# A fused attention and two-layer expert kernel: the seven-product blocks in another order, and the layer's inputs loaded during the last expert

## The chip, the cores and the metric

The kernel runs on one core of a Trainium2 chip. The metric is the device time of one execution in microseconds (us). The core has a matrix engine (TensorE, PE in the profile), VectorE (DVE), ScalarE (ACT), GpSimd (POOL) and a queue engine that issues transfers (SP). Each engine runs its instructions strictly in the order in which the program hands them to it, and engines wait for each other by semaphores.

## The reference

Three steps on 1536 tokens of 512 numbers. Local attention gives `x`. A mixture of eight experts follows: every token goes to the expert with the highest gate value, through `relu(x @ w1[e]) @ w2[e]`, and is scaled. Last comes a gated layer without a nonlinearity, and it is this one that the change is about:

```python
def _moe2_ref(x, w_a, w_b, w_out) -> np.ndarray:
    a = x @ w_a            # 1536 x 512 times 512 x 1536
    b = x @ w_b
    return (a * b @ w_out).astype(np.float32)
```

Everything is float32.

## The kernel before, in words

**Precision.** Each float32 matrix is split into a high and a low part (`h`, `l`), and a product is three matmuls: high times high, high times low, low times high. A split is a cast on ScalarE (the high part) and a subtraction on VectorE or GpSimd (the low part).

**Experts.** `for k, n in enumerate(CAPS)` goes through eight experts, k=7 the last. An expert has eight `up` and four `down` products; between them `tick(i)` issues side work for the step i = 0 to 15: loads and splits of later weights (`wstep`, `eload`, `esplit`), and by the table `CV` the first loads and conversions of the last layer's weights. The tokens are sorted by expert, and each expert's results are written transposed to a DRAM scratch `y_dram`. The weights' tiles rotate through pools: of twelve consecutive weight jobs four use pool A and eight pool B.

**The last layer.** Its 1536 tokens are three chunks c = 0, 1, 2 of 512, its 1536 hidden units twelve blocks f of 128. For f = 0 and 1 every chunk is multiplied directly: `first()` does chunk 0 (48 matmuls into the four banks `N0`) as soon as the experts are through, then `plain(c, f, ...)` does chunks 2 and 1. For f = 2 to 11 `seven(f)` computes chunks 0 and 1 together: as two-by-two blocks (a and b against two halves of the inner dimension, times two chunks) with seven products instead of eight, six matmuls each. The seven are, by their operands: `A11`, `S2`, `S1`, `A12`, `S3`, `A22` and `S4`; S1 to S4 are sums of the inputs, T1 to T4 (from `tsum` on VectorE, split by `tsplit` on ScalarE and GpSimd) sums of the weights. Partial sums meet in the banks `pa`, `pb`, `pc` and in the tiles `p1`, `u2`, `u3`. `ab2(0)` and `ab2(1)` are chunk 2's direct products, twelve matmuls each. `gate(c, f, ...)` splits a*b into `gh` (ScalarE) and `gl` (VectorE, when the function that it returns is called).

**Output.** Two neighbouring blocks f are a pair p. `both(p)` puts the pair's twelve output tiles (three chunks of four tiles of 128 tokens) on a list; `fill(n)` takes n tiles off it, each of six matmuls against the output weights in a bank of tag `o` (three of them), then an addition into the accumulator on VectorE (for the first pair a copy, on VectorE or ScalarE by turns).

**Weights.** `JOBS` lists half blocks of weights: for each f two of them, and from f = 2 to 10 one of the output weights (`WO`). A job is loaded by `cload` into one of three stage tiles (SP's queue), unpacked from float64 by `conv1` (two ScalarE operations), `conv2` (three VectorE operations and a GpSimd addition, which frees the stage tile) and split by `conv3` (ScalarE's cast, GpSimd's subtraction). Block f converts the jobs of f+1, `jobs` and `wo`, and loads and unpacks those of f+2, `nxt`.

**The branch.** `with tc.If(rare[0] == 1)` stands between the experts and the last layer: if an expert has more tokens than its capacity, the rest is computed there and the layer's inputs are loaded and prepared again. With these inputs it is not taken, but all five engines go through it, and instructions behind it wait for semaphores that stand in for the branch's own work.

**Order.** The whole program is under `tc.manual_schedule()`: on each engine the order is that of the Python statements. Before the change `xload()` (L1018) loads all three chunks, six transfers of 512 KB, between the last expert and the branch, into `acc`, a tile of a pool that takes the memory of the closed weight pools.

Of the kernel before, what the change touches and what calls it, by code (L numbers as in the profile page):

```python
# [46 lines left out]
def moe_block_kernel(ctx, tc, qd, kd, vd, kt, vn, nv, wg, wg2, we, wm, out):  # L47
# [41 lines left out]
    wA = ctx.enter_context(tc.tile_pool(name="wA", bufs=4))  # L89
    sts = ExitStack()  # L90
# [579 lines left out]
    pools["B"] = wbs.enter_context(tc.tile_pool(name="wB", bufs=8, side="left", reuse_waits="tile"))  # L670
# [64 lines left out]
    def down(W, d, Hm, n, col, pool, bg=None, d0=0, w=CMAX, q=nc.scalar, tag=("h", 6)):  # L735
        Ws = [[x[:, :].rearrange("p (f n) -> p f n", f=2)[:, f % 2, d * P:(d + 1) * P] for x in W(4 + f // 2)] for f in range(8)]
        pp = product(Ws, Hm, n, "ps_y", 255, bg, tag)
        yt = pool.tile([P, w], F32, tag="yt", bufs=4, name="yt")[:, 0:n]
        A.copy(yt, pp[-1])
        if len(pp) == 2:  # L740
            V.tensor_tensor(yt, pp[0], yt, ALU.add)  # L741
        return lambda: q.dma_start(y_dram[d0 + d, :, ds(col, n)], yt)

# [184 lines left out]
    for k, n in enumerate(CAPS):  # L928
# [8 lines left out]
        def tick(i):  # L937
# [28 lines left out]
            for f_, x in CV.get((k, i), ()):  # L966
                f_(x)

# [40 lines left out]
    acc = m1.tile([P, NT, DM], F32, name="acc")  # L1009
    XF = {(c, g): acc[:, 4 * c + 2 * g:4 * c + 2 * g + 2] for c in range(3) for g in range(2)}  # L1010

# [3 lines left out]
    Y2, S4, A22, S1, S2, S3 = (pair(m1, n_, k) for n_, k in (("Y2", 4), ("S4", 2), ("A22", 2), ("S1", 2), ("S2", 2), ("S3", 2)))  # L1015
    A11, A12 = ([y[:, a:a + 2] for y in yT] for a in (0, 2))

    def xload():  # L1018
        for c in (2, 1, 0):
            for g in range(2):  # L1020
                nc.sync.dma_start(XF[c, g], y_dram[2 * g:2 * g + 2, :, c * 512:(c + 1) * 512].rearrange("d p n -> p d n"))

# [7 lines left out]
    xload()  # L1030
    for h, l in (Y2, S4, A22):
        A.copy(h[:, 0, 0:2], ident[:, 0:2])
        V.tensor_copy(l[:, 0, 0:2], ident[:, 0:2])


    with tc.If(rare[0] == 1):
        with ExitStack() as ls:
# [76 lines left out]
            xload()  # L1114
            for g in range(2):
                ysp(XF[0, g], [y[:, 2 * g:2 * g + 2] for y in yT], V)
            first()
# [62 lines left out]
    def out_tile(p, c, t_):  # L1180
# [25 lines left out]
    def seven(f):  # L1206
# [3 lines left out]
        p1, u2, u3 = tmp("p1"), tmp("u2"), tmp("u3")  # L1210
# [5 lines left out]

        def conv_a():
            if jobs:
                conv2(*jobs, *wo)
                for _ in nxt:  # L1220
                    cload(nc.sync)

        def conv_b():
            for j in jobs + wo:
                conv3(j)
            if jobs:
                tsplit(f + 1)

        def ab2(s_):
            pt = bank("ab", 2)  # L1230
            mul(pt, wab(f, s_), Y2, True)
            if s_ == 0:
                A.copy(a, pt)
            else:
                V.tensor_tensor(pt, a, pt, ALU.mult)
                return gate(2, f, pt)

        def p4():
            mul(pb, T4, A22, False, True, True)
            V.tensor_tensor(p1, pb, p1, ALU.add)  # L1240
            V.tensor_tensor(pb, p1, u3, ALU.mult)
            return gate(1, f, pb)

        def p3():
            mul(pc, wab(f, 1, 2, 4), S4, False, True, True)
            V.tensor_tensor(u2, pc, u2, ALU.add)
            V.tensor_tensor(pa, u2, pa, ALU.mult)
            return gate(0, f, pa)
# [3 lines left out]
        conv_a()  # L1252
# [3 lines left out]
        mul(pa, wab(f, 0, 2, 4), A12, False, True, True)  # L1256
        if f % 2:
            ab2(0)
        else:
            fill(2)  # L1260
            if jobs:
                tsum(f + 1)
            fill(2)
            conv_b()
        mul(pb, T3, S3, False, True, True)
        V.tensor_tensor(u3, pb, p1, ALU.add)
        V.tensor_tensor(u3, u3, pc, ALU.add)
        if f % 2:
            if jobs:
                tsum(f + 1)  # L1270
            conv_b()
            low2 = ab2(1)
            low1 = p4()
            low2()
            low0 = p3()
            low1()
            low0()
            for j in nxt:
                conv1(j)
            both(f // 2)  # L1280
            fill(6 if f < 11 else 12)
        else:
            fill(2)
            for j in nxt:
                conv1(j)
            low1 = p4()
            low0 = p3()
            low1()
            low0()
            ab2(0)  # L1290
            ab2(1)()
# [3 lines left out]

    def ssum(o, a, b, op):
        V.tensor_tensor(o, a, b, op)


    def c12(*js):  # L1300
        for j in js:
            conv1(j)
        conv2(*js)
        for _ in js:
            cload(nc.sync)

    c12((12, 0), (12, 1))
    for g in range(2):
        ysp(XF[2, g], [y[:, 2 * g:2 * g + 2] for y in Y2], V)
    evict(0, 0, (N0[0, 0], N0[0, 1]), (), [(conv3, (12, 0)), (ysp, XF[1, 0], S4, V)])  # L1310
    evict(0, 1, (N0[1, 0], N0[1, 1]), (), [(conv3, (12, 1)), (ysp, XF[1, 1], A22, V)])
# [3 lines left out]
    plain(2, 0, ("o", "pc"), [(ssum, XF[1, 1], XF[1, 0], XF[1, 1], ALU.add)],  # L1315
          [(conv1, (2, 0)), (conv1, (2, 1)), (ssum, XF[1, 0], XF[0, 0], XF[1, 0], ALU.subtract)])
    plain(2, 1, ("pa", "pb"), [(conv2, (2, 0), (2, 1)), (cload, nc.sync), (cload, nc.sync)],
          [(ssum, XF[0, 0], XF[1, 1], XF[0, 0], ALU.subtract)])
    plain(1, 0, pab, [(ysp, XF[0, 0], S2, V), (tsum, 2)], [(conv3, (2, 0)), (ssum, XF[0, 1], XF[0, 1], XF[0, 0], ALU.subtract)])
    plain(1, 1, ("o", "pc"), [(conv3, (2, 1)), (tsplit, 2)], [(ysp, XF[1, 1], S1, V)])  # L1320
    both(0)
    ysp(XF[0, 1], S4, V)
    fill(2)
    ysp(XF[1, 0], S3, V)
    fill(4)
    c12((13, 0))
    conv3((13, 0))
    for j in ((3, 0), (3, 1), (13, 1)):
        conv1(j)
    for f in range(2, 12):  # L1330
        seven(f)
# [45 lines left out]
```

## Time and profile before

| | |
|---|---|
| three runs | 623.5, 624.6 and 625.32 us; median 624.6 |
| the profiled execution | 625.51 us, its span 623.8 us, mean granted TensorE clock 0.962 |
| TensorE matmul, busy | 574.1 us, 92% of the span |
| VectorE / ScalarE / GpSimd, busy | 442.2 / 307.7 / 255.2 us |
| DMA | 87.24 MB, mean 140 GB/s |

Times of a row are us from the span's start. A duration is that of one instruction or, with xN, of N merged ones from the first's start to the last's end; instructions on one engine overlap a little at their ends. A bracket `[2.10 <-DVE ...]` is the engine's idle time ahead of the row and what ended it. Matmul ends are modelled. In the rows by stage, the number behind the stage is its length, then busy time and count for each engine, and PEclk is the granted TensorE clock as a share of 2.4 GHz, a mean over the stage.

### The profile page before, as it was taken

How to read it: one execution, taken by the hardware profiler on the slowest of the kernel's cores; microseconds unless marked ns; L12 is line 12 of the kernel's file. 1: busy time of each engine (PE TensorE's matmuls, PEld its weight loads, DVE VectorE, ACT ScalarE, POOL GpSimd, SP SyncE). 2: the span in 40 equal slices, each digit the busy share in tenths (PEclk: the TensorE clock that was granted, in tenths of full speed). 3: DMA queues.
4: the chain of work that ended last, by engine and by line, in shares of the span. 5: the costliest groups of instructions: out<-in, count | busy, mean ns of one | idle time of the engine just before them, and what ended most of it. 6: DMA issues, size and time to landing. Idle time of an engine off the chain costs nothing.

```text
span 623.8 us, 9972 instructions
## 1 busy us (share of the span) xinstructions
PE 574.1 (92%) x3395; PEld 485.8 (78%) x3395; DVE 442.2 (71%) x987; ACT 307.7 (49%) x684; POOL 255.2 (41%) x227
## 2 busy tenths in 40 slices
PE   6998995799999999899979769899999989989995
PEld 4876774799999989889858558678778868868884
DVE  6888886696645868678358567777778678587463
ACT  5786881466566766686245345334234244242110
POOL 3000641543535636454413343743625517346115
PEclk9999997599999999999989779999989989999998
DMA  8476575467657796773831030221303203110004
GB/s 282 148 216 240 170 216 163 145 206 249 222 180 261 226 327 213 238 250 122 285 112 69 0 134 1 101 65 37 102 1 102 100 2 101 35 66 1 0 30 174
DMA packets 38656, 87.24 MB, mean 140 GB/s; under 512 B 5920, under 2 KB 16416, under 8 KB 38592
## 3 DMA queue, kind: packets, MB, share of 16 engines
q1 hardware_dynamic: 31680, 73.55, 36.3%
q0 software_dynamic: 2160, 6.91, 3.1%
q10 hardware_dynamic: 4752, 6.00, 2.9%
q8 instruction: 31, 0.51, 0.4%
q14 instruction: 33, 0.27, 0.1%
HBM read 73.25 MB, written 13.20 MB: 139 GB/s over the span
## 4 chain that ended last, share of the span: by engine, by line
PE 38%; DVE 6%; issue 3%; ACT 1%; POOL 1%; DMA 1%; POOLq 0%; ACTq 0%
PE ps_o L1187 5%; PE ps_o L1185 5%; PE ps_o L1186 5%; PE ps_ab L990 3%; PE ps_ab L989 3%; PE ps_ab L991 3%; PE ps_pb L990 2%; PE ps_pb L989 2%; PE ps_pb L991 2%; PE ps_pa L989 2%; PE ps_pa L991 2%; PE ps_pa L990 2%; PE ps_pc L989 1%; PE ps_pc L991 1%; PE ps_pc L990 1%
## 5 line engine op out<-in xcount | busy, mean ns | idle before, releaser
L886 POOL TENSOR_TENSOR tx<-tx,st 128x512 int32<-128x512 int32 x36 | 57.9, 1633 | 121.6 <-issue 93.1
L110 POOL TENSOR_TENSOR wl<-st,wh 128x512 fp32r<-128x512 f32 x54 | 69.2, 1302 | 91.8 <-ACT wh L105 85.5
L105 ACT CAST wh<-st 128x1024 fp32r<-128x1024 f32 x64 | 67.4, 1054 | 32.5 <-DMA st<-we 31.8
L110 DVE TENSOR_TENSOR wl<-st,wh 128x1024 fp32r<-128x1024 f32 x37 | 53.2, 1439 | 26.7 <-ACT wh L105 26.6
L719 PE MATMUL ps_h<-x,wl 128*128 128x256 f32 (+5 forms) x256 | 69.7, 272 | 0.0
L719 PE MATMUL ps_y<-h,wl 128*128 128x256 f32 (+5 forms) x256 | 68.6, 268 | 0.0
L1187 PE MATMUL ps_o<-wh,gl 128*128 128x512 f32 x144 | 59.7, 415 | 5.2 <-DVE gl L1151 5.2
L1185 PE MATMUL ps_o<-wh,gh 128*128 128x512 f32 x144 | 60.3, 418 | 4.6 <-ACT acc L1190 2.0
L898 POOL TENSOR_TENSOR wl<-tx,wh 128x512 fp32r<-128x512 f32 x36 | 49.5, 1405 | 27.8 <-ACT wh L897 27.8
L1186 PE MATMUL ps_o<-wl,gh 128*128 128x512 f32 x144 | 59.3, 412 | 0.0
L1192 DVE TENSOR_TENSOR acc<-ps_o,acc 128x512 f32<-128x512 f32 x60 | 39.9, 686 | 26.7 <-PE ps_o L1187 26.7
L515 ACT ACTIVATE pe<-pe,mx 128x256 f32<-128x256 f32 (+1 forms) x96 | 45.9, 480 | 22.0 <-DVE mx L511 22.0
L715 PE MATMUL ps_y<-h,wh 128*128 128x448 f32 (+3 forms) x160 | 50.4, 373 | 3.3 <-DVE h L733 2.8
L719 PEld LDWEIGHTS ps_h<-x,wl 128*128 128x128 f32 x256 | 49.8, 194 | 0.0
L715 PE MATMUL ps_h<-x,wh 128*128 128x448 f32 (+3 forms) x160 | 48.1, 365 | 0.9 <-DVE yt L741 0.9
L719 PEld LDWEIGHTS ps_y<-h,wl 128*128 128x128 f32 x256 | 48.5, 190 | 0.0
L1185 PEld LDWEIGHTS ps_o<-wh,gh 128*128 128x128 f32 x144 | 28.5, 198 | 15.4 <-ACT gh L1150 3.4
L1187 PEld LDWEIGHTS ps_o<-wh,gl 128*128 128x128 f32 x144 | 28.5, 198 | 13.8 <-DVE gl L1151 6.9
L511 DVE CUSTOM_DVE_ANT_0 pe<-ps_s,bias 128x256 f32<-128x256 f32 (+1 forms) x96 | 32.8, 398 | 7.4 <-PE ps_s L505 6.4
L715 PEld LDWEIGHTS ps_y<-h,wh 128*128 128x128 f32 x160 | 30.0, 188 | 6.5 <-issue 1.9
L1139 POOL TENSOR_TENSOR wl<-tt,wh 128x512 fp32r<-128x512 f32 x20 | 28.1, 1428 | 15.6 <-ACT wh L1137 15.6
L733 DVE SCALAR_TENSOR_TENSOR h<-ps_h,h 128x256 fp32r<-128x256 f32 (+5 forms) x64 | 24.8, 393 | 13.1 <-ACT h L728 11.7
(321 smaller groups left out, 1542.6 us busy)
## 6 DMA issues: line engine op xcount, KB each, us to landing
st<-we SPq DMA_DIRECT2D x63, 512.0 KB, 4.5
st<-wm SPq DMA_DIRECT2D x32, 512.0 KB, 4.7
vc<-vd SPq DMA_DIRECT2D x16, 352.0 KB, 4.0
k<-kd SPq DMA_DIRECT2D x7, 464.0 KB, 5.6
y_dram<-zero SPq DMA_DIRECT2D x12, 256.0 KB, 5.7
x_dram<-x SPq DMA_DIRECT2D x6, 512.0 KB, 4.1
acc<-y_dram SPq DMA_DIRECT2D x6, 512.0 KB, 7.4
q<-qd SPq DMA_DIRECT2D x7, 384.0 KB, 6.0
```

Of the source, the lines that this page charges most:

```text
L105: A.copy(wh, st)
L110: eng.tensor_tensor(wl[:, r], st[:, r], wh[:, r].bitcast(F32), ALU.subtract)
L715: T.matmul(pt[:, 0:2 * n].rearrange("p (s n) -> p s n", s=2), a, M[:, k], start=(k == 0), stop=False)
L719: T.matmul(pt[:, 0:n], b, M[:, k, 0], start=False, stop=(k == last))
L886: lambda t=txi, l=l: G.tensor_tensor(t, t, l, ALU.add)))
L898: G.tensor_tensor(wl_, tx, wh.bitcast(F32), ALU.subtract)
L989: T.matmul(pt, wh[:, k, :], yh[:, k, :], start=start and k == 0, stop=False, skip_group_check=more)
L990: T.matmul(pt, wh[:, k, :], yl[:, k, :], start=False, stop=False, skip_group_check=more)
L991: T.matmul(pt, wl[:, k, :], yh[:, k, :], start=False, stop=stop and k == n - 1, skip_group_check=more)
L1185: T.matmul(po, gh, wh, start=(i == 0), stop=False)
L1186: T.matmul(po, gh, wl, start=False, stop=False)
L1187: T.matmul(po, gl, wh, start=False, stop=(i == 1))
```

## The change

Four things change, and the number of matmuls does not.

1. Eight tiles of 4 KB a partition (`big`) become a pool of their own. Weight jobs 4 to 7 of twelve use it (pool B keeps the other four), and when expert k = 7 runs, four of these tiles take chunks 1 and 0, loaded at the steps i = 2 to 5 of that expert. Chunk 2 is loaded behind the experts, into the same pool; S4 lies there too. Output sums are kept in the six tiles of the loaded chunks instead of `acc`.
2. The splits of the inputs S4 and A22, the four sums of the inputs and `conv1`, `conv2` and two loads for the first output weights move ahead of the branch. Chunk 1 is multiplied ahead of chunk 2 in the plain blocks.
3. In `seven` the order of products is A11, S2, S1, (chunk 2's first half or four output tiles), A12, (its second half or two tiles), S3, S4, A22; before, A22 came ahead of S4. `conv2` of the output weights' job, `tsum`, `tsplit`, `conv3` and the loads stand together in `side()`; `conv1` of the next jobs goes behind the gates.
4. The sum for chunk 1 is built with one operand in PSUM (v = pc + p1, v = pb + v, then pb = pb + p1 and pb = pb * v in the bank) instead of a product of the two SBUF tiles p1 and u3 (L1240, L1241).

The core of the diff:

```diff
+    bgp = ctx.enter_context(tc.tile_pool(name="bg", bufs=8, reuse_waits="tile"))
+    def big(name, dt=F32):
+        return bgp.tile([P, 1024], dt, tag="bg", bufs=8, name=name)
...
+    XL = {2: (1, 0), 3: (1, 1), 4: (0, 0), 5: (0, 1)}
+    def xload(c, g):
+        if (c, g) not in XF:
+            XF[c, g] = big("acc")[:, :].rearrange("p (k n) -> p k n", k=2)
+        nc.sync.dma_start(XF[c, g], y_dram[2 * g:2 * g + 2, :, c * 512:(c + 1) * 512].rearrange("d p n -> p d n"))
...
+            if k == NE - 1 and i in XL:
+                xload(*XL[i])
...
-    xload()
-    for h, l in (Y2, S4, A22):
+    for g in range(2):
+        xload(2, g)
+    ysp(XF[1, 0], S4, V)
+    ysp(XF[1, 1], A22, V)
+    for h, l in (Y2, S2, S1, S3):
         A.copy(h[:, 0, 0:2], ident[:, 0:2])
         V.tensor_copy(l[:, 0, 0:2], ident[:, 0:2])
+    sums()
+    c12((12, 0), (12, 1))
     with tc.If(rare[0] == 1):
...
+        def side():
+            if jobs:
+                tsum(f + 1)
+                tsplit(f + 1)
+                conv2(*wo)
+                for j in jobs + wo:
+                    conv3(j)
+                for _ in nxt:
+                    cload(nc.sync)
         mul(pa, wab(f, 0, 0, 2), A11, True)
         A.copy(p1, pa)
-        conv_a()
+        conv2(*jobs)
         mul(pb, T2, S2, True)
         V.tensor_tensor(u2, pb, p1, ALU.add)
         mul(pc, T1, S1, True)
-        mul(pa, wab(f, 0, 2, 4), A12, False, True, True)
+        V.tensor_tensor(v, pc, p1, ALU.add)
         if f % 2:
             ab2(0)
         else:
+            fill(4)
+        side()
+        mul(pa, wab(f, 0, 2, 4), A12, False, True, True)
+        if f % 2:
+            ab2(1)
+            low[2]()
+        else:
             fill(2)
         mul(pb, T3, S3, False, True, True)
+        V.tensor_tensor(v, pb, v, ALU.add)
+        mul(pc, wab(f, 1, 2, 4), S4, False, True, True)
+        V.tensor_tensor(u2, pc, u2, ALU.add)
+        V.tensor_tensor(pa, u2, pa, ALU.mult)
+        low[0] = gate(0, f, pa)
+        mul(pb, T4, A22, False, True, True)
+        V.tensor_tensor(pb, pb, p1, ALU.add)
+        V.tensor_tensor(pb, pb, v, ALU.mult)
+        low[1] = gate(1, f, pb)
+        low[0]()
+        low[1]()
+        for j in nxt:
+            conv1(j)
...
+    c12((2, 0), (2, 1))
+    plain(1, 0, ("o", "pc"), (), [(tsum, 2), (conv3, (2, 0)), (conv3, (2, 1))])
+    plain(1, 1, ("pa", "pb"), (), [(tsplit, 2), (ysp, XF[0, 0], S2, V)])
+    plain(2, 0, pab, [(ysp, XF[1, 1], S1, V)], [(ysp, XF[0, 1], S4, V)])
+    plain(2, 1, ("o", "pc"), [(ysp, XF[1, 0], S3, V)])
     c12((13, 0))
-    conv3((13, 0))
     for j in ((3, 0), (3, 1), (13, 1)):
         conv1(j)
+    both(0)
+    fill(6)
+    conv3((13, 0))
     for f in range(2, 12):
         seven(f)
```

## Rows read from the trace of the kernel before

**Rows 1.** Busy time by stage: N0's end to f=2, then f=2 to f=5.
```profile
311.82:354.13 42.31, 35.44 (x134) 27.60 (x134) 29.07 (x37) 20.46 (x31) 12.50 (x8) 0.88 0.20 67
354.13:384.88 30.75, 25.60 (x104) 20.42 (x103) 18.05 (x28) 15.53 (x27) 13.52 (x10) 0.89 0.20 69
384.88:410.81 25.93, 24.24 (x103) 18.91 (x102) 19.92 (x31) 9.38 (x16) 11.67 (x8) 1.00 0.18 61
410.81:434.33 23.52, 23.52 (x103) 19.09 (x102) 18.02 (x29) 8.68 (x14) 11.46 (x8) 1.00 0.20 67
434.33:461.59 27.26, 25.56 (x104) 20.09 (x102) 20.11 (x31) 9.41 (x16) 11.67 (x8) 0.94 0.19 59
```

**Rows 2.** Waits of TensorE, 311 to 612 us: total, times, longest.
```profile
PE ps_o L1187 <- DVE gl L1151: 5.2, 4, 1.3
PE ps_pa L989 <- ACT p L1251: 5.2, 1, 5.2
PE ps_o L989 <- ACT Y2h L1026: 3.1, 1, 3.1
...
PE ps_o L1185 <- ACT gh L1150: 1.6, 4, 0.4
```

**Rows 3.** Timeline of ScalarE in block f=2.
```profile
361.87 0.66 ACT L869 ACTIVATE tx<-st 128x512 f32<-128x512 f32 x1 [0.37 <-DMA st<-wm]
...
362.99 0.56 ACT L1251 COPY p<-ps_pa 128x512 f32<-128x512 f32 x1
```

**Rows 4.** Timeline of VectorE: tsum's first step alone, then block f=5.
```profile
337.84 0.42 DVE L1129 TENSOR_TENSOR tt<-tx 128x256 f32<-128x256 f32 x1
...
436.56 1.09 DVE L881 TENSOR_SCALAR tx<-tx 128x512 f32<-128x512 f32 x3
...
440.38 0.68 DVE L1254 TENSOR_TENSOR u<-ps_pb,p 128x512 f32<-128x512 f32 x1
...
445.50 1.46 DVE L1129 TENSOR_TENSOR tt<-tx 128x256 f32<-128x256 f32 x1
...
450.30 1.76 DVE L1241 TENSOR_TENSOR ps_pb<-p,u 128x512 f32<-128x512 f32 x1
...
452.57 0.67 DVE L1246 TENSOR_TENSOR u<-ps_pc,u 128x512 f32<-128x512 f32 x1
```

**Rows 5.** Timeline of ScalarE, block f=5.
```profile
449.10 1.05 ACT L1137 CAST wh<-tt 128x1024 fp32r<-128x1024 f32 x1 [4.08 <-DVE tt L1132]
450.06 0.57 ACT L1150 CAST gh<-ps_ab 128x512 fp32r<-128x512 f32 x1
...
454.49 0.68 ACT L869 ACTIVATE tx<-st 128x512 f32<-128x512 f32 x1
```

**Rows 6.** Timeline of GpSimd: two additions of conv2, two subtractions of tsplit.
```profile
306.31 2.89 POOL L886 TENSOR_TENSOR tx<-tx,st 128x512 int32<-128x512 int32 x2 [2.10 <-DVE tx L884]
...
425.11 2.57 POOL L1139 TENSOR_TENSOR wl<-tt,wh 128x512 fp32r<-128x512 f32 x2 [1.78 <-ACT wh L1137]
```

**Rows 7.** Timeline of SP's queue at the last expert's end.
```profile
300.02 1.81 SPq L742 DMA_DIRECT2D y_dram<-yt  x2
```

**Rows 8.** Groups of VectorE by line and shape: busy, mean ns, idle before.
```profile
L1297 DVE TENSOR_TENSOR acc<-acc 128x1024 f32<-128x1024 f32 x4 | 5.4, 1343 | 0.0
L1028 DVE TENSOR_TENSOR Y2l<-acc,Y2h 128x1024 fp32r<-128x1024 f32 x2 | 2.4, 1222 | 8.1 <-ACT Y2h L1026 8.1
L1028 DVE TENSOR_TENSOR S1l<-acc,S1h 128x1024 fp32r<-128x1024 f32 x1 | 1.5, 1518 | 2.2 <-ACT S1h L1026 2.2
```

**Rows 9.** Instructions of the branch's line L1036 on SP: durations, first and last start.
```profile
L1036 SPq EVENT_SEMAPHORE  x9: 17/17/17, 313.3 to 316.2; - x9
...
L1036 SPq COMPARE_BRANCH  x1: 50/50/50, 308.2 to 308.2; - x1
```

**Rows 10.** Waits of ScalarE, 300 to 612 us.
```profile
ACT Y2h L1026 <- SPq L1036: 8.8, 1, 8.8
```

**Rows 11.** Line L862, loads of the last layer's weights: time to landing.
```profile
DMA to landing us min/median/max: 3.1/4.7/5.7
```

More of the change, by code (lines that the diff above doesn't have):

```diff
@@ L1113, in moe_block_kernel @@
             lqs.close()
-            xload()
+            for c in (1, 0, 2):
+                for g in range(2):
+                    xload(c, g)
             for g in range(2):
                 ysp(XF[0, g], [y[:, 2 * g:2 * g + 2] for y in yT], V)
+            ysp(XF[1, 0], S4, V)
+            ysp(XF[1, 1], A22, V)
+            sums()
             first()
@@ L1215, in seven @@
         a = tmp("a")
[L1217 to L1227, printed above, removed]
+        low = {}
         def ab2(s_):
@@ L1235, in ab2 @@
                 V.tensor_tensor(pt, a, pt, ALU.mult)
[L1236 to L1248, printed above, removed]
+                low[2] = gate(2, f, pt)
+        def side():
[6 more added lines that the diff above has]
+                for _ in nxt:
+                    cload(nc.sync)
         mul(pa, wab(f, 0, 0, 2), A11, True)
         A.copy(p1, pa)
-        conv_a()
+        conv2(*jobs)
         mul(pb, T2, S2, True)
@@ L1259, in seven @@
         else:
+            fill(4)
[5 more added lines that the diff above has]
+        else:
             fill(2)
[L1261 to L1264, printed above, removed]
         mul(pb, T3, S3, False, True, True)
-        V.tensor_tensor(u3, pb, p1, ALU.add)
-        V.tensor_tensor(u3, u3, pc, ALU.add)
-        if f % 2:
[L1269 to L1279, printed above, removed]
+        V.tensor_tensor(v, pb, v, ALU.add)
[10 more added lines that the diff above has]
+        for j in nxt:
+            conv1(j)
+        if f % 2:
             both(f // 2)
@@ L1282, in seven @@
         else:
[L1283 to L1289, printed above, removed]
             ab2(0)
-            ab2(1)()
+            ab2(1)
+            low[2]()
     def both(p):
         items.extend((p, c, t_) for c in (2, 0, 1) for t_ in range(4))
[L1296 to L1311, printed above, removed]
+    evict(0, 0, (N0[0, 0], N0[0, 1]), (), [(conv3, (12, 0))])
+    evict(0, 1, (N0[1, 0], N0[1, 1]), (), [(conv3, (12, 1))])
     pse.close()
@@ L1314, in moe_block_kernel @@
     pab = [bank("ab", 2) for _ in range(2)]
[L1315 to L1325, printed above, removed]
+    for g in range(2):
+        ysp(XF[2, g], [y[:, 2 * g:2 * g + 2] for y in Y2], V)
+    c12((2, 0), (2, 1))
[3 more added lines that the diff above has]
+    plain(2, 1, ("o", "pc"), [(ysp, XF[1, 0], S3, V)])
     c12((13, 0))
-    conv3((13, 0))
     for j in ((3, 0), (3, 1), (13, 1)):
         conv1(j)
+    both(0)
+    fill(6)
+    conv3((13, 0))
     for f in range(2, 12):
```

40 lines of the change are left out of this document (25 added, 15 removed).

## The prediction

> **What bounds the kernel now.** I read the page's busy times first: TensorE has work for nearly all of the span, so the reader looks for the places where it has none. The change touches the second layer and the load ahead of it, so next comes busy time and granted clock of that layer block by block [rows 1], then who releases TensorE there [rows 2]. A pair of hidden blocks is an even and an odd one, with 102 matmuls each. An even block from f=4 on takes 23.5 us, with TensorE busy all the time at full clock: 0.23 us a matmul. Nothing but a smaller matmul count could shorten it, and the change leaves every count as it is. What can be won stands in the other rows: f=2 takes 30.75 us, 7.25 over an even block; f=3 takes 25.93 and f=5 27.26 (f=9 is like the former, f=7 like the latter), together 12.3 us over four even blocks; and the stretch from the last matmul of chunk 0 to f=2 takes 42.31 us for 132 matmuls, 30.4 at 0.23, so 11.9 over. That is 31.4 us in all.
>
> Who ends the waits: in f=2 ScalarE's copy of p1 (5.15 us), in the four odd blocks the gate's two parts (1.6 and 5.2 us over four places), at the stretch's start Y2 (3.1 us) [rows 2]. f=2's copy is late because ScalarE stands before it at a conversion whose load had just landed [rows 3]. In an odd block the gate is late because VectorE runs tsum beside GpSimd's subtractions, 1.46 us instead of the 0.42 it takes alone, and then a product of two SBUF tiles, 1.76 us [rows 4].
>
> **The time the sum stands on.** The profiled execution took 625.51 us, 0.9 above the median of 624.6; the sum is made against it and 0.9 taken off at the end.
>
> **Part 1, block f=2: 7.25 us less.** conv1 of (3,0), (3,1) and (13,1) moves ahead of the six output tiles, so p1 is copied on time, and the wait of 5.15 us and the slow clock behind it go. Next late would be VectorE's sum of S3; it has some 3 us of slack, as in the even walk below. Bounds: 4 to 7.25 us.
>
> **Part 2, the even blocks: nothing.** Walk f=4 in the new order, from its first matmul. Four tiles end at 42 matmuls, 9.7; the last add frees VectorE at 10.4; tsum alone 1.55, to 12.0; three conversions to 13.5; two adds to 14.8. S3 ends at 60 matmuls, 13.8 plus 1.5, at 15.3, when VectorE is free, and A22 follows six matmuls later, so the addition of v hides in S4. Its ScalarE casts end at 17.7, before the gate needs them at 18.2. What is lost is lost at the end: conv1 now stands ahead of the copy of ab2(0), six ScalarE operations of 0.6 to 0.7 us [rows 5] behind a gate that ends at 20.2, so the block's last gate comes about 0.5 us later than before.
>
> **Part 3, the odd blocks f=3, 5, 7, 9: the wait moves, and grows.** The old gap goes: v is built with one operand in PSUM, and such an operation takes 0.67 us also beside GpSimd (L1246) where the SBUF product takes 1.76 [rows 4]. But side() puts the conversion of the third job, conv2(wo), behind tsplit's two subtractions on GpSimd, and its cast in front of ab2(1)'s gate on ScalarE. Behind that gate VectorE's low part waits, behind it (one queue, in order) v = pb + v, and pb may not be added to by A22 until v has read it. From the block's first matmul:
> - VectorE starts conv2 at 2.7 (2.23 before, and the 0.5 of part 2). Nine such operations took 3.82 us, 0.42 each [rows 4]; the fifth gives GpSimd its first operand at 4.8.
> - GpSimd adds two tiles, 2.9 us [rows 6], to 7.7; tsum, now without GpSimd beside it, 1.55 [rows 4], to 9.3; ScalarE's cast 1.05 [rows 5], to 10.4; GpSimd's two subtractions 2.57 [rows 6], to 13.0; its add for the third job 1.3, half of a pair without overlap, to 14.3.
> - ScalarE's cast of it 0.6, the gate 0.57 [rows 5], to 15.5; VectorE's low part and v, 0.7 each, to 16.9; with the hand-overs 17.0.
> TensorE reaches A22 after 60 matmuls, 13.8. So it waits 3.2 us, where it waited 1.7 by the row of waits, and 2.0 with the starts beside it. From below: 2.2 (conv2 at 2.2, every hand-over free); from above 5.3, with tsum as slow as beside GpSimd. After A22 nothing new is late: four tiles of chunk 2, 5.6 us, lie between it and the first gate that it feeds.
> The clock adds to a wait: f=3 lost 2.4 us at clock 1.00, f=5 lost 3.75 at 0.94 for the same gaps, and f=2 lost 7.25 for one of 5.15 [rows 1, 2]. What the rows show there is TensorE's clock at its lower level, 1.2 instead of 2.4 GHz, for a while behind a gap. So a wait of about 2 us costs 0.4 to 1.7 on top, one of 5 costs 2.1; for 3.2 I take 1.5. That makes 4.7 us a block, 18.8 for the four, against 12.3: **6.5 us more** (bounds 1.9 less to 17 more). f=11 has no third job and no wait.
>
> **Part 4, from the last expert to f=2: 2.6 us more.** Four of six loads move into the last expert. Their queue (SP) carries the last weights before them and the first output of that expert behind them; the last output, done with at 301.8 [rows 7], sets chunk 2's loads and is not moved. Chunk 1 goes first after chunk 0, so TensorE no longer waits for Y2. What it waits for is VectorE's way to the branch: from 303.1 two splits (2.7), four sums of about 1.15, and six conversions (2.6) [rows 4, 8], to 313.1, and some 0.5 for the branch. TensorE starts at 313.6, where it started at 314.9 and waited once more, and the gap is too short to expect the slow clock: up to 4 us early, and nothing on VectorE yet.
> Then the branch. Before, SP stood there until its loads had landed (events from 313.3 to 316.2) and ScalarE's Y2h waited for it, 8.8 us [rows 9, 10]. Now c12((12,0),(12,1)) stands ahead of the branch: its conversions end at 313, GpSimd's adds at 315.5, and only then SP issues the second of two loads, which takes 3.1 to 5.7 us to land [rows 11]. So SP's events come at about 319.6 and Y2h at 320, 6 us later than before. From there ScalarE and VectorE go hand in hand through the rest, in program order: Y2's two splits and conv2 to 326; mult 0.7; tsum, beside GpSimd's subtractions for (2,0) and (2,1), 3.5 us as in f=5 instead of 1.55, with 1.8 of wait before it; gl and the next mult to 333; gate, tsplit, S2h on ScalarE 2.6; then four splits of 1.2 to 1.5 [rows 8], two mults, three low parts and two waits of 1.5 for ScalarE. The last low part of chunk 2 comes at 346. TensorE has done its 96 matmuls by 335.6 and needs it for the first output tile: it stands until 345.6. Then 31 matmuls (7.2), the slow clock behind such a gap (2.3), and a wait of 1.6 for ScalarE, which holds tile 1's copy behind conv1((13,1)) and its load: f=2 starts at 356.7 instead of 354.1. Bounds: 5 us less (SP free at 314, tsum alone) to 6 more (both loads slow).
>
> A rule bears on this part. The rows: tsum's first step 1.46 us beside GpSimd, 0.42 alone [rows 4]. The Trainium skill (SBUF — State Buffer, Who interferes with whom) says that a VectorE instruction with two SBUF inputs and a GpSimd instruction that reads SBUF exclude each other for the whole instruction, the one that starts first holding on. It speaks against this part, since tsum now stands beside subtractions where it stood alone: by it the stretch is 1.9 us longer than with tsum at 1.55, as in the sum.
>
> **Sum.** -7.25 + 6.5 + 2.6 = +1.9: 627.4 us for a profiled execution, 626.5 against the median. What is won in f=2 is lost again in the odd blocks and ahead of f=2.
>
> **Rivals.**
> A. The odd blocks have no wait, as the order of side() is meant to give. For it: GpSimd is busy for under half of an odd block [rows 1]. Against: the queues' order in the walk. Then 625.5 - 7.25 - 12.3 + 2.6 = 608.5, 607.6 as a median.
> B. The wait is there but at its low end without the clock falling, 2.2 + 0.4 us: 4 x 2.6 = 10.4, 8.4 under the forecast, 618.
> C. The stretch gains: SP's events do not hold Y2h beyond 314. For it: the two loads that Y2h reads are issued long before those two. Against: the same events held it in the run before [rows 10]. It gives -5 instead of +2.6, 619.
> D. Slower: SP's branch costs what it cost before, 5.1 us from branch to first event, with a landing of 5.7 behind it. Y2h comes at 325 instead of 320, and since ScalarE and VectorE are serial from there on, each us is a us of the end: 632. It decides from Y2h at about 322 on.
>
> **How the numbers follow.** The forecast has 0.56, with its own range from 620 to 633 (odd wait 2.6 to 4.2 us, stretch -1 to +5). A 0.12, B 0.09, C 0.10, D 0.13. 0.3% of 624.6 is 1.9 us, about what can be told from no change: below 622.7 faster, above 626.5 slower. The forecast lies on the upper edge: of its 0.56 some 0.07 falls below, 0.21 between, 0.28 above. Faster 0.07 + 0.12 + 0.09 + 0.10 = 0.38, same 0.21, slower 0.28 + 0.13 = 0.41. The range from 612 to 635 leaves out A and little above.
>
> **What would show it.** In the new profile: f=2 at about 23.6 us, no wait for p; in f=3, 5, 7, 9 a wait of about 3 us ahead of T4 times A22, released by VectorE's v (the second line of that name), and in front of the gate gh2 a ScalarE wait for GpSimd's tx; none at the output tiles. Between 335 and 346 TensorE stands for the gate of chunk 2, and Y2h is released by SP near 320. It is wrong if odd blocks come out near 23.5, if f=2 keeps a gap, or if it starts before 352.

## The result, and the profile after

The changed kernel takes 632.81 us (median of four runs, 632.1 to 634.16) against 624.96 us of the kernel before on the same chip (623.5 to 625.52): a ratio of 1.0132, 95% interval 1.0107 to 1.0157. A second measurement with more rounds gave 631.97 against 624.51 us, 1.0125 (1.0096 to 1.0153). It is slower by 7 to 8 us. The forecast was 626.5 us with 612 to 635 as its range, and a chance of 0.41 for slower.

The profiled execution took 632.77 us, its span 631.1 us, 7.3 us more than the span before. By stage (columns as in [rows 1]):

```profile
310.76:357.87 47.11, 36.21 (x133) 27.73 (x134) 29.12 (x45) 23.38 (x37) 15.86 (x11) 0.86 0.17 57
357.87:381.37 23.50, 23.50 (x104) 19.12 (x102) 12.02 (x21) 10.42 (x18) 11.61 (x9) 1.00 0.20 68
381.37:409.72 28.35, 25.32 (x103) 20.21 (x102) 17.44 (x31) 9.95 (x18) 10.62 (x8) 0.94 0.17 56
409.72:433.20 23.48, 23.48 (x103) 19.11 (x102) 16.09 (x29) 7.60 (x13) 10.71 (x8) 1.00 0.20 67
433.20:461.63 28.43, 25.32 (x103) 20.20 (x102) 17.43 (x31) 10.03 (x18) 10.60 (x8) 0.94 0.17 56
...
537.05:566.73 29.68, 26.57 (x104) 21.16 (x103) 17.43 (x31) 10.06 (x18) 10.59 (x8) 0.88 0.17 53
...
605.67:631.10 25.43, 16.96 (x73) 13.28 (x71) 10.80 (x16) 1.10 (x2) 11.79 (x12) 0.88 0.32 124
```

Read against [rows 1]: f=2 (second row) has lost its gap, f=4 (fourth) is what it was, and the odd blocks f=3, 5 and 9 are longer, f=9 most, at the same wait and a lower clock. The last row runs from the last block's first output product to the end of the span; before, that took 23.41 us. (Its clock of 0.88 comes from the time behind 625 us, where it is 0.51; up to there it is 1.00.) Where the 7.3 us come from, each from the starts of TensorE's matmuls:

| part | before | after | difference | forecast |
|---|---|---|---|---|
| start of f=2 | 354.13 | 357.87 | +3.7 | +2.6 |
| f=2 | 30.75 | 23.50 | -7.25 | -7.25 |
| f=3, 5, 7, 9 together | 106.37 | 114.92 | +8.55 | +6.5 |
| f=4, 6, 8, 10 together | 94.07 | 93.94 | -0.1 | 0 |
| f=11 up to its outputs | 15.07 | 15.44 | +0.4 | 0 |
| from there to the end of the span | 23.41 | 25.43 | +2.0 | 0 |

The first row holds two things. From N0's first matmul (300.57 before, 299.50 after) to f=2 the changed kernel takes 58.37 us instead of 53.56, 4.8 more; but N0 itself began 1.1 us earlier. In the second profile of the changed kernel N0 begins at 301.06 and f=2 at 359.65.

TensorE's waits from 300 to 620 us, with the total, the times and the longest:

```profile
PE ps_pb L1007 <- DVE v L1292: 12.4, 4, 3.1
PE ps_o L1221 <- ACT gh L1186: 6.2, 2, 4.7
PE ps_o L1223 <- DVE gl L1187: 1.9, 1, 1.9
PE ps_o L1008 <- DVEq L1067: 1.5, 1, 1.5
```

The first row is new, once in each odd block: A22's first product may not add to the bank until v = pb + v has read it. The others lie ahead of f=2. The waits for p, for Y2h and the eight small ones at the output products [rows 2] are gone.

The chain behind the first row in block f=5, on VectorE, ScalarE and GpSimd:

```profile
444.47 0.70 DVE L1260 TENSOR_TENSOR ps_ab<-a,ps_ab 128x512 f32<-128x512 f32 x1 [0.43 <-PE ps_ab L1009]
448.85 0.69 DVE L1187 TENSOR_TENSOR gl<-ps_ab,gh 128x512 fp32r<-128x512 f32 x1 [3.68 <-ACT gh L1186]
449.46 0.68 DVE L1292 TENSOR_TENSOR v<-ps_pb,v 128x512 f32<-128x512 f32 x1
```

```profile
442.55 1.05 ACT L1173 CAST wh<-tt 128x1024 fp32r<-128x1024 f32 x1 [1.65 <-DVE tt L1168]
...
447.72 0.62 ACT L913 CAST wh<-tx 128x512 fp32r<-128x512 f32 x1 [3.08 <-POOL tx L902]
448.24 0.58 ACT L1186 CAST gh<-ps_ab 128x512 fp32r<-128x512 f32 x1
```

```profile
443.68 2.76 POOL L1175 TENSOR_TENSOR wl<-tt,wh 128x512 fp32r<-128x512 f32 x2 [2.75 <-ACT wh L1173]
446.40 1.29 POOL L902 TENSOR_TENSOR tx<-tx,st 128x512 int32<-128x512 int32 x1
```

Read from the bottom: GpSimd comes to the output weight's addition only at 446.40, behind tsplit's two subtractions; ScalarE stands 3.08 us for it, and gh, whose bank was ready at 445.2, is behind it in the queue; gl waits 3.68 us for gh, and v, whose products had ended at about 445.7, is behind gl. Three queues, each in its own order, hand one delay along to a TensorE that needs none of the first two results yet.

Ahead of f=2, the events with which four engines leave the branch, and ScalarE:

```profile
L1067 SPq EVENT_SEMAPHORE  x9: 17/17/17, 319.7 to 320.8; - x9
...
L1067 DVEq EVENT_SEMAPHORE  x2: 21/21/21, 313.1 to 313.3; - x2
L1067 POOLq EVENT_SEMAPHORE  x2: 17/17/17, 315.6 to 315.7; - x2
```

```profile
315.60 0.58 ACT L1192 COPY a<-ps_n 128x512 f32<-128x512 f32 x1 [10.00 <-POOLq L1067]
...
320.47 2.00 ACT L1037 CAST Y2h<-acc 128x1024 fp32r<-128x1024 f32 x2
...
340.76 0.58 ACT L1186 CAST gh<-ps_ab 128x512 fp32r<-128x512 f32 x1 [2.91 <-DVE ps_ab L1194]
```

ScalarE waits 10 us for GpSimd's event, not for SP's (the x9 row), and the gate that the first output product needs comes at 340.76, when TensorE has been idle since 336.7.

The end of the span, VectorE's last additions, before (one row) and after (four):

```profile
617.48 0.69 DVE L1192 TENSOR_TENSOR acc<-ps_o,acc 128x512 f32<-128x512 f32 x1 [0.71 <-PE ps_o L1187]
```

```profile
618.47 0.69 DVE L1228 TENSOR_TENSOR acc<-ps_o,acc 128x512 f32<-128x512 f32 x1 [0.71 <-PE ps_o L1223]
620.95 0.69 DVE L1228 TENSOR_TENSOR acc<-ps_o,acc 128x512 f32<-128x512 f32 x1 [1.79 <-PE ps_o L1223]
622.41 0.69 DVE L1228 TENSOR_TENSOR acc<-ps_o,acc 128x512 f32<-128x512 f32 x1 [0.77 <-PE ps_o L1223]
625.28 0.69 DVE L1228 TENSOR_TENSOR acc<-ps_o,acc 128x512 f32<-128x512 f32 x1 [2.18 <-remote]
```

Up to 618.47 they come every 1.40 us, in the kernel before to the last one; here the last three are 1.1, 1.1 and 2.6 us late. The instruction DRAIN in TensorE's queue ends where the last addition begins (614.0 + 3.45 before, 619.2 + 6.07 after); it is the longer of the two in each of these rows, whose durations are in ns, shortest, median and longest:

```profile
L1373 PEldq DRAIN  x2: 13/1732/3452, 614.0 to 623.3; - x2
```

```profile
L1376 PEldq DRAIN  x2: 13/3040/6067, 619.2 to 630.5; - x2
```

### The profile page after: what moved, and what is told of

Read it like the earlier page. It is cut to its first block, busy times and chain, and to the rows that moved or that the text cites. A ratio compares the mean times of both kernels' runs of the same rounds, so it can differ in the third digit from the quotient of the medians.

```text
span 631.1 us, 9995 instructions
## 1 busy us (share of the span) xinstructions
PE 575.5 (91%) x3395; PEld 488.9 (77%) x3395; DVE 419.8 (67%) x988; ACT 307.0 (49%) x685; POOL 246.9 (39%) x227
## 5 line engine op out<-in xcount | busy, mean ns | idle before, releaser
L902 POOL TENSOR_TENSOR tx<-tx,st 128x512 int32<-128x512 int32 x36 | 51.5, 1444 | 115.4 <-ACT p L1274 54.2
L914 POOL TENSOR_TENSOR wl<-tx,wh 128x512 fp32r<-128x512 f32 x36 | 47.3, 1336 | 19.6 <-ACT wh L913 9.4
L1221 PEld LDWEIGHTS ps_o<-wh,gh 128*128 128x128 f32 x144 | 28.8, 200 | 15.5 <-ACT gh L1186 7.2
L913 ACT CAST wh<-tx 128x512 fp32r<-128x512 f32 x36 | 21.3, 619 | 28.5 <-POOL tx L902 28.5
L1222 PEld LDWEIGHTS ps_o<-wl,gh 128*128 128x128 f32 x144 | 28.9, 201 | 7.0
```

Of the source, the lines that this page charges most:

```text
L902: lambda t=txi, l=l: G.tensor_tensor(t, t, l, ALU.add)))
L914: G.tensor_tensor(wl_, tx, wh.bitcast(F32), ALU.subtract)
L1221: T.matmul(po, gh, wh, start=(i == 0), stop=False)
L1222: T.matmul(po, gh, wl, start=False, stop=False)
```

## Experiments

Times are medians; "before" is the kernel before in the same rounds on the same chip (624.2 to 624.5 us). Stages are from each run's own profile. "Stretch" is from N0's first matmul to f=2: 53.56 us before, 58.37 changed, 58.59 in the changed kernel's second profile. N0's first matmul itself comes at 298.0 to 301.1 us in the thirteen profiles, 1.6 us apart in the two of the changed kernel, so that differences of that size between two spans can lie ahead of it. Some of the expectations below name stretches up to 2.1 us shorter: they count from the first matmul behind 300 us, which is not always N0's first. "Odd" is f=3, 5, 7 and 9 together.

**Each half alone.** The first run has the changed kernel's loads, branch and transition with the blocks of before.

```diff
     def seven(f):
...
-        p1, u2, v = tmp("p1"), tmp("u2"), tmp("v")
+        p1, u2, u3 = tmp("p1"), tmp("u2"), tmp("u3")
...
-        conv2(*jobs)
+        conv_a()
...
```

> The changed kernel with the seven-product blocks of before (order, u3 and the gate over p1): the early loads, the two splits and sums ahead of the branch and the new order from N0 to f=2 alone. Theory (the blocks carry the loss, the transition pays for itself): odd blocks f=3, 5, 7, 9 back at 106.4 us in sum (114.9 changed); N0's end to f=2 stays at +3.7 us against before; f=2 keeps most of its -7.25 us, since its loss before came from the first converts that stood ahead of p1's copy on ScalarE, and those are moved by the transition; together -3.5 us, 621 to 622.5 us, ratio about 0.995. Rival (the new order in f=2 itself made the gain): f=2 at about 30 us, 629 us. For the 2.0 us at the end of the span (last additions at 620.95, 622.41, 625.28): if they belong to the new blocks they are gone here; if to the transition or to no edit they stay, and the time is 2 us above either figure.

622.09 us, ratio 0.9962 (0.9935 to 0.9990). Stretch 58.88, f=2 23.50, odd 107.74, and the end 23.5 us. In its rows, f=2 and f=3:

```profile
357.58:381.08 23.50, 23.50 (x103) 19.12 (x102) 12.84 (x21) 10.95 (x19) 12.06 (x9) 1.00 0.20 68
381.08:408.29 27.21, 25.56 (x103) 20.11 (x102) 20.07 (x31) 9.40 (x16) 11.64 (x8) 0.94 0.16 58
```

The transition costs 5.3 us in the stretch and wins 7.25 in f=2; from N0's first matmul to the end this profile is only 0.4 us shorter than before, and N0 itself begins 1.9 us earlier (298.70). Whether that earlier start belongs to the loads in the last expert, no run here tells. The odd blocks' loss belongs to the new blocks. The second run has the other half: the kernel before, with `seven` as changed.

```diff
     def seven(f):
...
+        conv2(*jobs)
         mul(pb, T2, S2, True)
...
+            fill(4)
+        side()
...
```

> The kernel before with the changed seven-product blocks alone; loads, branch and transition as before. Theory: odd blocks f=3, 5, 7, 9 114 to 115 us in sum as in the changed kernel (106.4 before), even blocks 23.5 each, N0's end to f=2 42.3 us as before, f=2 still long, 29 to 31 us (ScalarE comes to p1's copy late as before); in sum +8.5 us, 632.5 to 635 us, ratio 1.014. Rival (the wait in the odd blocks comes from where the transition leaves the queues, a lag that is carried from block to block): odd blocks at 106 us, 624 to 626 us. Tail: with the new blocks 25.4 us from the last block's first output product to the span's end, else 23.4 us.

625.76 us, ratio 1.0024 (0.9999 to 1.0049): the odd blocks as expected, 114.62, but f=2 far shorter than expected, and the time with it:

```profile
350.88:376.19 25.31, 23.77 (x103) 19.07 (x102) 15.56 (x28) 14.93 (x26) 13.28 (x10) 1.00 0.24 84
376.19:404.39 28.20, 25.16 (x103) 20.12 (x102) 17.34 (x31) 9.99 (x18) 10.59 (x8) 0.94 0.17 56
```

ScalarE copies p1 as late as before, 9.0 us into f=2 (359.86), but in the new order four output tiles stand between p1's product and A12's, which overwrites its bank: TensorE does not wait for p. So either half takes f=2's gap away, and their gains do not add: -7.25 and -5.4 alone, -7.25 together. Its stretch of 51.31 us, 2.2 under the kernel before with the same statements there, is not an effect of the edit: the run below with the same transition has 53.60.

**The odd blocks' wait.** First the output weight's cast is moved.

```diff
-                for j in jobs + wo:
+                for j in jobs if f % 2 else jobs + wo:
                     conv3(j)
...
             ab2(1)
             low[2]()
+            for j in wo:
+                conv3(j)
```

> The changed kernel, but in odd blocks the cast and low part of the output weight (conv3 of wo) come behind gh and gl of the third gate instead of ahead of ab2(1). Theory: in f=5 gh at 448.24 was held by that cast, which waits 3.1 us for GpSimd's addition (446.40, behind the two subtractions of tsplit); without it gh starts at about 445.2, right after the multiply at 444.47, gl ends at 446.5, v at 447.1, and T4's products start 0.2 to 0.5 us late instead of 3.1. Each odd block 23.5 to 24.2 us, f=3, 5, 7, 9 94 to 97 us in sum instead of 114.9; 613 to 615 us, ratio to before 0.981 to 0.984. Rival 1 (the low clock in these blocks has another cause than the wait): 25.3 us of busy time stay, 102 us in sum, 620 us. Rival 2 (another wait takes its place: the output products wait for gl of the first chunk, or the first products of the next block for p1): 26 to 28 us each, 624 to 631 us.

611.35 us, ratio 0.9792 (0.9765 to 0.9820); odd 95.42, each 23.85. ScalarE in f=5, and the stage:

```profile
442.25 0.59 ACT L1186 CAST gh<-ps_ab 128x512 fp32r<-128x512 f32 x1 [0.57 <-DVE ps_ab L1260]
444.79 0.62 ACT L913 CAST wh<-tx 128x512 fp32r<-128x512 f32 x1 [1.95 <-POOL tx L902]
```

```profile
430.25:454.10 23.85, 23.77 (x103) 19.04 (x102) 17.43 (x31) 10.16 (x18) 10.70 (x8) 1.00 0.20 67
```

gh starts as its multiply (441.52, 0.69) ends; the cast still waits for GpSimd, with nobody behind it in a hurry. Without the wait the granted clock is 1.00 in every odd block, here and under the second cure, so the slow clock was the wait's. The second cure leaves ScalarE alone and moves gl behind v on VectorE.

```diff
             ab2(1)
-            low[2]()
...
         V.tensor_tensor(pa, u2, pa, ALU.mult)
+        if f % 2:
+            low[2]()
```

> The changed kernel, but in odd blocks VectorE takes the low part of the third gate (gl, low[2]) behind v, u2 and the multiply of pa instead of ahead of them; ScalarE's order, with the output weight's cast ahead of gh, stays. Theory (A22's products waited only because v stands behind gl on VectorE): gh stays at 448.2, v starts when S3's products end at 445.7, T4's products start on time; gl ends at about 449.5, so that the first output products wait 0.5 to 1.5 us for it; odd blocks 24 to 25 us, 96 to 100 us in sum, 614 to 618 us. Rival (ScalarE's late gh takes the wait along to the output products): 3 us again, 26 to 28 us each, 625 to 631 us.

613.35 us, ratio 0.9839 (0.9808 to 0.9871); odd 95.90. VectorE in f=5:

```profile
441.74 0.69 DVE L1291 TENSOR_TENSOR v<-ps_pb,v 128x512 f32<-128x512 f32 x1 [0.59 <-PE ps_pb L1009]
...
444.84 0.69 DVE L1187 TENSOR_TENSOR gl<-ps_ab,gh 128x512 fp32r<-128x512 f32 x1 [0.32 <-ACT gh L1186]
```

gh is as late as ever (444.23), v is not, and A22's products start on time at 442.90. The price that was expected at the output products is 0.5 us a block at most. One link of the chain is enough; which one does not matter much.

**The branch.** c12((12,0),(12,1)) goes back behind it, to where it stood.

```diff
     sums()
-    c12((12, 0), (12, 1))
     with tc.If(rare[0] == 1):
...
+    c12((12, 0), (12, 1))
     evict(0, 0, (N0[0, 0], N0[0, 1]), (), [(conv3, (12, 0))])
```

> The changed kernel with the converts and two loads c12((12,0),(12,1)) behind the branch again, right ahead of the two gates of N0, where they stood before. Theory: they hold the branch of three queues: VectorE's at 311.9, GpSimd's at 313.2 (its event at 315.6 releases ScalarE's first copy, 10.0 us of wait), SP's at 315.9 (its events at 319.7). Without them ScalarE's first copy starts once N0 and its converts are done, 310 to 312 instead of 315.60, TensorE's 2.0 us before the second product of plain(1,0) go to under 0.5, and the 4.7 us before the first output product shrink to 1 to 3; N0's end to f=2 3 to 5 us shorter, the rest as it was: 628 to 630 us, ratio 1.005 to 1.008. Rival (the stretch hangs on VectorE's tsum beside GpSimd's subtractions and on the two sums ahead of the branch, not on the events): f=2 starts within 1 us of 357.9 and the time stays at 632 to 633 us.

626.99 us, ratio 1.0048 (1.0025 to 1.0071); stretch 54.61, 3.8 less. ScalarE's start, and TensorE's longest wait there:

```profile
309.98 0.59 ACT L1191 COPY a<-ps_n 128x512 f32<-128x512 f32 x1 [3.73 <-PEq L1066]
...
316.65 2.00 ACT L1037 CAST Y2h<-acc 128x1024 fp32r<-128x1024 f32 x2
```

```profile
PE ps_o L1220 <- ACT gh L1185: 6.6, 2, 5.0
```

Y2h comes 3.8 us earlier, 2.9 counted from N0's first matmul, so c12 ahead of the branch cost 3.8 of the 4.8 us that the stretch lost. The wait ahead of the first output product was expected to shrink and did not: it is another loss, which the kernel before did not have at that place. To see which queue held ScalarE, the two loads alone went behind the branch, converts and additions staying ahead.

```diff
-    c12((12, 0), (12, 1))
+    for j in ((12, 0), (12, 1)):
+        conv1(j)
+    conv2((12, 0), (12, 1))
     with tc.If(rare[0] == 1):
...
+    for _ in range(2):
+        cload(nc.sync)
```

> The changed kernel with only the two loads of c12((12,0),(12,1)) moved behind the branch; its converts and GpSimd's additions stay ahead of it. Theory 1 (GpSimd's additions hold the branch: its event at 315.6 releases ScalarE's first copy, and ScalarE comes to Y2h at 320.4 by its own order): SP's branch and events come 4 to 6 us earlier, but ScalarE's first copy stays at 315 to 316 and N0's start to f=2 at 57 to 58.6 us; 631 to 633 us, ratio 1.011 to 1.014. Theory 2 (the prediction's: SP's events hold Y2h): Y2h goes out at 314 to 316, N0's start to f=2 at 52 to 54.5 us; 627 to 629 us.

631.1 us, ratio 1.0111 (1.0070 to 1.0152); stretch 58.44.

```profile
L1069 SPq EVENT_SEMAPHORE  x9: 17/17/17, 310.2 to 310.8; - x9
...
L1069 POOLq EVENT_SEMAPHORE  x2: 17/17/17, 314.7 to 314.8; - x2
```

```profile
314.75 0.59 ACT L1194 COPY a<-ps_n 128x512 f32<-128x512 f32 x1 [10.04 <-POOLq L1069]
...
319.46 2.00 ACT L1037 CAST Y2h<-acc 128x1024 fp32r<-128x1024 f32 x2
```

SP's events come 9.5 us earlier and nothing follows; ScalarE is let go by GpSimd's, as before. By that row the two additions of c12 hold the branch (in the changed kernel GpSimd stands 9.48 us ahead of them for VectorE's conversions), not the loads. The same run shows what the clock makes of one wait. All four odd blocks have it at 3.1 us, f=3 at full clock and f=5 not:

```profile
380.55:407.37 26.82, 23.77 (x103) 19.04 (x102) 17.33 (x31) 10.01 (x18) 10.61 (x8) 1.00 0.18 59
...
430.85:460.38 29.53, 26.41 (x103) 21.00 (x102) 17.42 (x31) 10.05 (x18) 10.61 (x8) 0.88 0.16 54
```

**Both cures, and the order ahead of f=2.** The late cast and c12 behind the branch:

> The changed kernel with the edits of the two runs before joined: in odd blocks the output weight's cast behind the third gate, and c12((12,0),(12,1)) behind the branch. Theory (the odd blocks' wait and the branch's held queues are two losses that do not touch): the gains add, 19.5 us in the odd blocks (95.4 in sum) and 4.5 us from N0's end to f=2 (53.0): 606 to 608 us, ratio 0.972. Rival (the odd blocks' work was waiting for the same loads, or the earlier start runs into them): 609 to 612 us.

610.69 us, ratio 0.9789 (0.9761 to 0.9818). Stretch 55.47 and odd 95.41, so in the stages the gains add (3.1 us in the stretch against the late cast alone, 58.56); yet the time is only 0.7 us lower, inside the uncertainty of either. In the profiles, the late additions at the end, which the late cast alone did not have, take 2.3 us back (25.33 against 23.01 us). The rest is within the spread of the runs (609.5 to 612.2). Then, in this kernel with both cures, tsum and most splits were taken out from between the gates:

```diff
-    plain(1, 0, ("o", "pc"), (), [(tsum, 2), (conv3, (2, 0)), (conv3, (2, 1))])
-    plain(1, 1, ("pa", "pb"), (), [(tsplit, 2), (ysp, XF[0, 0], S2, V)])
-    plain(2, 0, pab, [(ysp, XF[1, 1], S1, V)], [(ysp, XF[0, 1], S4, V)])
-    plain(2, 1, ("o", "pc"), [(ysp, XF[1, 0], S3, V)])
...
+    plain(1, 0, ("o", "pc"), (), [(c12, (13, 0))])
+    plain(1, 1, ("pa", "pb"), (), [(ysp, XF[0, 0], S2, V)])
+    plain(2, 0, pab)
+    plain(2, 1, ("o", "pc"), [(tsum, 2)])
+    tsplit(2)
+    ysp(XF[1, 1], S1, V)
+    both(0)
+    fill(2)
...
```

> The run with both edits joined, and the stretch from N0 to f=2 in another order: tsum(2), tsplit(2), the splits of S1, S4 and S3 and conv3 of (2,0), (2,1) come behind the gates of the last two plain products instead of between them; c12((13,0)) goes into the gate of plain(1,0). Theory (in the changed kernel the 4.7 us ahead of the first output product are VectorE's: tsum waits 1.9 us for GpSimd's addition and takes 1.5 and 1.4 us a step beside GpSimd's subtractions, and the multiplies of the next two gates stand behind it): the first output product starts within 1.5 us of the last plain one, TensorE reaches it at 333 to 335, f=2 starts at 342 to 345, the stretch from N0's start to f=2 42.5 to 45 us against 53.0; 597 to 600 us, ratio 0.956 to 0.96. Rival 1 (the moved work comes due at f=2: T2's low part or S2, S1 late): up to 6 us of new wait in f=2 and its first products, 602 to 606 us. Rival 2 (ScalarE's order, not VectorE's, sets the gates): the wait ahead of the outputs stays at 4 to 5 us, 606 to 608 us.

601.24 us, ratio 0.9644 (0.9614 to 0.9674); stretch 47.18, 8.3 less than with the two cures. tsum's first steps, in the changed kernel and here:

```profile
329.08 1.51 DVE L1165 TENSOR_TENSOR tt<-tx 128x256 f32<-128x256 f32 x1 [1.86 <-POOL tx L902]
330.63 1.40 DVE L1166 TENSOR_TENSOR tt<-tx,tt 128x256 f32<-128x256 f32 x1
```

```profile
332.76 0.42 DVE L1164 TENSOR_TENSOR tt<-tx 128x256 f32<-128x256 f32 x1
333.21 0.43 DVE L1165 TENSOR_TENSOR tt<-tx,tt 128x256 f32<-128x256 f32 x1
```

The first output product starts 0.7 us after the last plain one; a wait of 2.2 us stands ahead of the second, for the last gate, whose multiply is now behind tsum. That was tried away by moving tsum and S2's split behind it as well (the calls after `plain(2, 1, ...)`).

> The run with the late tsum, and now tsum(2) and the split of S2 also behind the multiply and the low part of the last plain product (there tsum stood ahead of that multiply, and the second output product waited 2.2 us for its gate). Theory (VectorE's order sets the gates): the last multiply at 332 to 333 instead of 334.2, the wait of 2.2 us goes to under 0.7, f=2 starts at 341 to 343, N0's start to f=2 41 to 43 us (45.1), 2 to 4 us less: 597 to 599.5 us, ratio 0.956 to 0.96. Rival (what was moved comes due in f=2: T2's low parts or S2l late): the stretch shrinks, but f=2 takes 25 to 28 us instead of 23.5, 600 to 602 us.

598.64 us, ratio 0.9607 (0.9566 to 0.9647), the lowest time here, though its interval overlaps that of the run before it; and not for the reason given. Stretch 47.33, f=2 23.49: nothing gained there. The waits of that stretch were and are, in the run before this one and in this one:

```profile
PE ps_o L1220 <- ACT gh L1185: 2.5, 2, 2.2
```

```profile
PE ps_o L1220 <- ACT acc L1225: 1.6, 1, 1.6
PE ps_o L1220 <- DVE acc L1225: 1.2, 1, 1.2
PE ps_o L1007 <- DVE tx L897: 1.0, 1, 1.0
PE ps_o L1220 <- ACT gh L1185: 0.8, 1, 0.8
```

Most of the wait for the gate became waits for the copies of the output tiles, which now stand behind the moved splits on ScalarE and VectorE. The span is 1.8 us shorter because this profile has no late additions at the end (22.9 us there against 25.3).

**What the early loads are worth.** The kernel before, with its own transition, and the changed blocks with the late cast:

> The kernel before with the changed seven-product blocks, in which odd blocks take the output weight's cast behind the third gate; loads, branch and transition of before. It asks what the changed transition is worth once the blocks are mended. Theory (the new blocks carry nearly all of the gain, and f=2's wait goes with them): f=2 25.3 us, odd blocks 95.4 in sum, N0's start to f=2 51 to 53.6 us: 606 to 610 us, ratio 0.972 to 0.977, no slower than the two edits joined with the changed transition (610.7). Rival (the early loads are worth their own 3 to 5 us): 612 to 615 us.

607.4 us, ratio 0.9729 (0.9691 to 0.9768); stretch 53.60, f=2 25.37, odd 95.41. No slower than the two cures joined with the changed transition (0.9789): from N0's first matmul to f=3 the one takes 78.97 us, the other 78.98. With the transition as it stands and the late cast (0.9792) it is 82.06. So the changed transition brings nothing that the mended blocks do not bring by themselves, and costs 3 us as it stands. With its order ahead of f=2 repaired, in the run with the late tsum, that way takes 70.68 us. No run has that order with the loads of before, so whether the early loads are needed for it stays open.

**The changed kernel again.**

> The changed kernel itself once more. Its first profile has 25.4 us from the last block's first output product to the end of the span (23.4 before), with the last three additions at 620.95, 622.41 and 625.28 instead of every 1.40 us. If that belongs to the change it is here again, 632 to 634 us; if it came by chance in that one execution, additions every 1.40 us, 23.4 us, and 630 to 632 us.

631.97 us; the last additions again at 622.71, 624.15 and 626.96, late by the same steps. So the changed kernel has the late end in both profiles.

## Why the prediction was right in kind and 6 us short

**f=2: right in size, incomplete in cause.** -7.25 forecast and measured. The forecast gave it to the conversions that moved ahead of the output tiles; the first run shows that they suffice, the second that the new order of products all but suffices too.

**Even blocks: right.** They take 23.5 us as before. Behind them conv2 of the odd block starts 0.45 us later (2.67 us from its first matmul, before 2.23), as said.

**Odd blocks: the walk right to 0.25 us, the clock's share too small.** Block f=5, us from its first matmul (433.20):

| step | forecast | measured |
|---|---|---|
| conv2 on VectorE | 2.7 | 2.7 |
| GpSimd's first addition | 4.8 | 4.8 |
| two additions done | 7.7 | 7.7 |
| tsum done | 9.3 | 9.3 |
| tsplit's cast done | 10.4 | 10.4 |
| its two subtractions done | 13.0 | 13.2 |
| output weight's addition done | 14.3 | 14.5 |
| gate gh done | 15.5 | 15.6 |
| v read, A22 free | 17.0 | 17.0 |

The wait was put at 3.2 us and is 3.1. The step that was mis-sized is "for 3.2 I take 1.5": over an even block, TensorE's busy time is 1.8 us longer in f=3, 5 and 7 and 3.1 in f=9, 2.15 on average. Four times 5.25 instead of 4.7 is 2.2 us more, the whole of what this term is short by (2.05 in the table above; its even blocks are 0.1 us shorter than before). The rows of before [rows 1] could not have given it better than as a spread: in the run with the loads behind the branch one wait of 3.1 us cost 0.3 us on top in f=3 and 2.9 in f=5.

**Last expert to f=2: 1.1 us more than forecast, 3 in the second profile, one link wrong.** That it is only 1.1 owes something to luck: N0 began 1.1 us earlier in the first profile, which the sum did not have. The link is that Y2h waits for SP's events: these came at 319.7 (forecast 319.6) and Y2h at 320.47 (320), so the numbers look like a proof, but it was ScalarE's own queue that brought it there, let go by GpSimd's event at 315.6. The run with the loads behind the branch shows it: SP free at 310, Y2h still at 319.46. The forecast followed the addition on GpSimd to 315.5 and passed over that GpSimd has to leave the branch as well, and that ScalarE's first copy waits for it. Rival D, which let SP's branch decide, is out by the same run: Y2h at 325 is not what happened, and that its 632 us is the measured time is chance. Behind that the walk held: tsum waits 1.86 us (1.8) and takes 3.6 (3.5), the last low part ends at 347.2 (346), f=2 starts at 357.87 (356.7). TensorE's one wait until 345.6 came as three, of 4.7, 1.9 and 1.6 us, the last of them until 346.56. TensorE's gaps at the branch, called too short for the slow clock, were 0.45 and 1.54 us, and the clock did fall (0.51 from 314.4 to 317.9); TensorE waited for the gates afterwards all the same, from 336.7 on, so it cost nothing here. The Trainium skill (SBUF — State Buffer, Who interferes with whom), by which a VectorE instruction with two SBUF inputs and a GpSimd instruction that reads SBUF shut each other out, agrees with these rows: 1.51 and 1.40 us beside GpSimd's subtractions, 0.42 and 0.43 without them.

**The end of the span: not in the sum.** 2.0 us. The late additions are there in five of thirteen profiles (the changed kernel twice, both cures joined, the late tsum, gl behind v) and absent in the other eight, among them each half alone and each cure of the changed kernel but one. The two cures of the odd blocks differ in the place of a call, and one has it. TensorE's records run on at 0.23 us a matmul to 622.24 and the granted clock is 1.00, yet its DRAIN, 3.45 us long in the kernel before, takes 6.07 (5.9 to 6.4 us in the five profiles, 3.45 to 3.46 in the others), which says that it was TensorE that was late. The Trainium skill (Perfetto Trace Analysis, Tensor Engine Instruction) says that the end of a TensorE instruction is estimated, not observed; that fits, and leaves the reason open. It is no effect of the change that any run here could pin to a statement.

**f=11: 0.4 us**, not counted: "no third job and no wait". It has no third job, but A22's products still stand behind gl and v on VectorE: v ends at 604.12 and A22 starts at 604.18, some 0.2 us behind its turn. With gl behind v the block takes 15.08 us, as before (15.07); with the new order otherwise 15.44.

**Rivals.** A (no wait) is refuted by the wait row, and the cured runs show what it would have given: 611.35 us, with the transition as it is. B failed because the wait was 3.1 us and the clock fell, C because the stretch got longer and Y2h came at 320.47. The forecast's mechanism held in the blocks, and in the stretch but for that one link; its sum of +1.9 became +7.3 as three terms came out 1.1, 2.0 and 2.4 us higher (stretch, odd blocks, end and f=11 together). The rest of the 6.3 us is the 0.9 that the forecast took off for the median: the changed kernel's profiled run, 632.77 us, lies on its median. The time is at the upper edge of the forecast's own range, 620 to 633.

## What to carry to other kernels

When a block's side work is regrouped, follow each engine's queue in order through one block: a step that nobody needs yet stalls TensorE if a step that it does need stands behind it, here over three queues, and moving one call (the cast, or the low part) was worth 19 to 21 us of 632. Work put ahead of a branch delays the engines that wait, behind it, for the event of the one with the most to do (here ScalarE, 10.0 us for GpSimd's); ask of each engine, not of the obvious one, when it gets there. And two edits that each remove the same wait are worth it once: run each half alone before adding their gains.

## What was not expected of the hardware

A wait of the same 3.1 us left TensorE's granted clock at 1.00 in one block and at 0.94 or 0.88 in others of the same execution (26.82 and 29.53 us for f=3 and f=5 of one run). And the results of TensorE's last products can come up to 2.6 us behind its own records with no lower granted clock shown, in five profiles of thirteen, and by nearly the same steps in both profiles of the changed kernel; the cause was not found.
